# Attention's keys loaded late in the projections, and stores placed behind the last visit

## The chip, the cores and the metric

The kernel runs on one core of a Trainium2 chip. The metric is the device time in microseconds of one launch. Engines are named as in the profile: PE is TensorE (PEld its weight loads), DVE VectorE, ACT ScalarE, POOL GpSimd, SP SyncE; SPq and ACTq are the instruction queues of SP and ACT, from which DMAs are issued.

## What is computed

A transformer block with conditioning: 2048 tokens, width 512, 32 heads of 16, a hidden layer of 1792, all in float32.

```python
mod = silu(c) @ w_mod                      # six vectors: sa, ca, ga, sb, cb, gb
h = layernorm(x) * (1 + ca) + sa
q, k, v = split(h @ wqkv)                  # 32 heads of 16
p = softmax(q @ k.T / 4)                   # per head, 2048 x 2048
x = x + ga * ((p @ v) @ wo)
h = layernorm(x) * (1 + cb) + sb
out = x + gb * (gelu(h @ w1 + b1) @ w2 + b2)
```

## The kernel before

Heads are worked on in eight groups of four, tokens in four blocks of 512. One group with one block of queries is a unit `u` (32 in all). Float32 products are made of a rounded high part and a low remainder, so a projection of a block is 12 matmuls of 512 columns in `mm3` (line 303). Its `fill` list holds functions that are called between these 12 matmuls: with three entries, after matmuls 4, 8 and 12.

**First part** (to about 72 us). The loop over blocks `b` normalizes a block, transposes it, and makes the queries and keys of the first quarter of the heads (`proj_qk` with `k = 0`) and some rows of values (`proj_v`). Each projection returns a function `rest` that issues the store of its result to device memory (lines 456, 459, 481); it is called after the matmuls of the next projection. The queue that issues it is `st[0]`. At first that is ACT.

**Second part** (about 72 to 299 us). 33 projections are left, numbered here 0 to 32: nine of values and 24 `proj_qk` with `k` from 1 to 3. Between their matmuls run 97 *visits*, numbered 0 to 96. A visit computes score products for the softmax maxima of nine units, before attention starts: six matmuls (line 566, tiles `mx<-kt,qmx`), half of them read out by ACT (line 572) and half by DVE (line 575). Visits read queries from `qmx` (two buffers, six DMAs of 64 KB each per unit, line 508) and combined keys from `kt0` or `kt1` (`build_k`, line 497, six DMAs of 256 KB). The units come in the order 0, 1, 2, 3, 4, 5, 8, 6, 7. Visit 42 is the first of unit 4, visit 64 the first of unit 8, visit 74 the first of unit 6, visit 85 the first of unit 7. Unit 8 belongs to another group of heads, so `kt0` is built anew for it, from `kpm1` in device memory, which `pair_store` (line 456) writes after projections 11 and 15.

**Attention** (299 to 1404 us) needs `kq0`, the plain keys of the first heads (again six DMAs of 256 KB), and in each key tile four rows of ones (`one_rows`, line 533, two DMAs of 32 KB over two partitions). The rest of the time goes to the feed-forward layers.

All loads, and from projection 1 on all stores, are issued by SP, one after another in the order in which the code was written. A DMA is issued when its data and its buffer are ready, and, since there are eight completion counters which the DMAs take in turn, when the earlier DMA on its counter has landed. So a DMA that waits holds up all that stand behind it in SP's queue. Engines run their instructions in the order of the code too; nothing is reordered.

Of the kernel before, what the change touches and what calls it, by code (L numbers as in the profile page):

```python
# [35 lines left out]

FRONT = (0, 1, 2, 3, 4, 5, 8, 6, 7, 9)
NU1 = len(FRONT) - 1
VISIT = 3
OP0 = 1  # L40
OPN = 4
# [11 lines left out]
def block_kernel(ctx: ExitStack, tc: tile.TileContext, x, wqkv, wo, w1, b1, w2, b2, c, w_mod, out):  # L53
    nc = tc.nc
    te, ve, ac, gp, sy = nc.tensor, nc.vector, nc.scalar, nc.gpsimd, nc.sync
    ctx.enter_context(tc.manual_schedule())

    def pool(name, bufs=1, **kw):
        cm = tc.tile_pool(name=name, bufs=bufs, **kw)
        return cm, cm.__enter__()  # L60

    def close(cm):
        cm.__exit__(None, None, None)
# [86 lines left out]
    def load_x(b):  # L150
        for t in range(4):
            r0 = b * TB + t * P
            sy.dma_start(x_tile(b, t), x[r0 : r0 + P, :])
# [4 lines left out]
    def load_w(k, hold=lambda raw: None):  # L158
        if k < 4:
            raw = tpool.tile([P, 2, KC, P], F32, tag="wraw", name="wraw")  # L160
            hold(raw)
            for w in (1, 0):
                sy.dma_start(raw[:, w], wq_r[:, :, w * D + k * P : w * D + (k + 1) * P])
        else:
            raw = vraw
            hold(raw)
            for i in range(KC):
                sy.dma_start(raw[:, i], wq_r[:, i, 2 * D :])
        raws[k] = raw
# [5 lines left out]
    def split_w(k):  # L175
        raw = raws.pop(k)
        w_parts(k)
        for w in (1, 0):
            if k > 1:
                gp.tensor_copy(w_hi[k][:, w], raw[:, w])  # L180
            else:
                ac.activation(w_hi[k][:, w], raw[:, w], AF.Copy)
            gp.tensor_tensor(w_lo[k][:, w], raw[:, w], w_hi[k][:, w].bitcast(F32), op=ALU.subtract)
# [34 lines left out]
    def mod_cols(v, r, ps=None, f0=0, f1=KC):  # L218

        if ps is None:  # L220
            ps = bank()[:, : 2 * KC]
        for fc in range(f0, f1):
            te.matmul(ps[:, fc * 2 : fc * 2 + 2], r[:, fc * P : (fc + 1) * P], sel[:, :2], start=True, stop=True)
        p2 = ps.rearrange("p (f i) -> p f i", i=2)
        ve.tensor_scalar(modc[:, v, f0:f1, 0], p2[:, f0:f1, 0], 1.0, None, op0=ALU.add)
        ve.tensor_copy(modc[:, v, f0:f1, 1], p2[:, f0:f1, 1])

    def mod_store(r):

        ps = bank()  # L230
        te.matmul(ps[:2], sel[:, :2], r, start=True, stop=True)
        g = apool.tile([P, D], F32, tag="h32", name="grow", bufs=3)
        ac.activation(g[:2], ps[:2], AF.Copy)
        sy.dma_start(g_d, g[:2])
# [39 lines left out]
    def ln1(b):  # L274

        tiles = [x_tile(b, t) for t in range(4)]
        mv, rs = ln_stats(tiles)

        def rows():
            for t in range(4):  # L280
                ve.tensor_scalar(tiles[t], tiles[t], mv[:, t, 0:1], rs[:, t : t + 1],
                                 op0=ALU.subtract, op1=ALU.mult)
            return tiles

        return rows

    def ln1_t(b, tiles, between=lambda: None):
        hi = hpool.tile([P, KC, TB], FR, name=f"hThi{b}")
        lo = hpool.tile([P, KC, TB], FR, name=f"hTlo{b}")
        hT[b] = hi, lo  # L290
        tr, evac = transposed(tiles, hi, lo, 0, apool, lambda fc: bank_mx() if fc < KC - 1 else bank(), (ve, gp))
        pss = [tr(fc) for fc in range(KC - 1)]
        between()
        pss.append(tr(KC - 1))
        return lambda: [evac(fc, pss[fc]) for fc in range(KC)]
# [12 lines left out]
    st = [ac]  # L308
# [183 lines left out]
    def build_k(dst, src, g, t0=0, t1=S, parts=(0, 1, 2)):  # L492
        for i in parts:
            part = (0, 0, 1)[i]
            for a in range(2):
                r0 = a * 64 + i * DH
                sy.dma_start(dst[r0 : r0 + DH, :, t0:t1].bitcast(F32), heads(src, g, part, a, t0, t1))

    def load_k(g, tile):
        kst[g] = tile  # L500
        build_k(tile, qk_d[1][g // 2], g)
# [8 lines left out]
    def load_qm(u):  # L510

        qmx[u] = qmpool.tile([P, 2, TB], FR, tag="qmx", name="qmx", bufs=2)
        build_q(u, qmx[u])
# [16 lines left out]
    def one_rows(k):  # L530
        for a in range(2):
            r0 = a * 64 + KR
            sy.dma_start(k[r0 : r0 + 2].bitcast(F32), one_d[:, None, :].to_broadcast([2, 2, S]))

    mxs, left, vabs = {}, {}, {}

    mi = [NU1 * NM, NU1 * NM]

# [80 lines left out]
    rest = lambda: None  # L619

    def proj(f, *args):

        nonlocal rest
        r = f(*args)
        rest()
        rest = r

    for b in range(NB):
        if b == NB - 1:
            close(lcm)  # L630
            kcm, kpool = pool("kpool")
            kts = [kpool.tile([P, 2, S], FR, name=f"kt{i}") for i in range(2)]
            qmcm, qmpool = pool("qmpool")
            kpm[0], kpm[1] = kts
            load_qm(0)
            build_k(kts[0], kpm_d[0], 0, 0, 2 * TB)
            load_qm(1)
        if b:
            if b + 1 < NB:
                xn = ln1(b + 1)()  # L640
            if b + 2 < NB:
                load_x(b + 2)
        proj(proj_qk, b, 0, 1, (), None if b else first[1])
        if b == 1:
            load_w(1)
        if b == NB - 1:
            st[0] = sy
            rest()
            rest, st[0] = lambda: None, ac
            split_w(1)  # L650
        proj(proj_qk, b, 0, 0, (), None if b else first[0])
        if b == 0:
            xn = ln1(1)()
        if b == NB - 1:
            mod_store(mrow)
            break
        if b == 1:
            mod_cols(1, mrow)
        for _ in range(V_A[b][0]):
            proj(proj_v, *vitems.pop(0), (), len(vitems) == 15)  # L660
        ev = ln1_t(b + 1, xn)
        ev()
        for _ in range(V_A[b][1]):
            proj(proj_v, *vitems.pop(0))
        if b < 2:
            mrow = mod_rows(wms)
        if b == 0:
            wms = [load_wm(2, 0), load_wm(5, 1)]
# [8 lines left out]
    items = [(None, b, t) for b, t in vitems] + [(k, b, w) for k in range(1, 4) for b in range(NB) for w in (1, 0)]  # L677
    nv = len(vitems)

    half = [("V", 0), None]  # L680
    for n in range(1, 16 * NU1):
        half += [("V", n), ("U", n - 1)]
    half += [None, ("U", 16 * NU1 - 1)]
    slots = list(zip(half + [None], [None] + half))
    visits = -(-len(slots) // VISIT)
    led, todo = 0, []
    new = []

    def visit():
        nonlocal led  # L690
        for sl in slots[led : led + VISIT]:
            for a in range(2):
                if sl[a]:
                    new.extend(half_slot(*sl[a], a))
        led += VISIT

    for n, (k, b, w) in enumerate(items):
        if n == 1:
            close(acm)
            st[0] = sy  # L700
        if n == 0:
            build_k(kts[0], kpm_d[0], 0, 2 * TB, S)
        if n == 5:
            load_w(2)
        if n == 7:
            build_k(kts[1], kpm_d[0], 1)
            for t in kts:
                one_rows(t)
        if n == nv + 1:
            close(vwcm)  # L710
            kqcm, kqpool = pool("kqpool")
            kq = [kqpool.tile([P, 2, S], FR, name="kq0")]
            one_rows(kq[0])
            vgcm, vgpool = pool("vgpool", bufs=2)
            qcm, qpool = pool("qpool")
        if n == nv + 2:
            load_k(0, kq[0])
        if n == nv + 10:
            kpm[2] = kts[0]
            build_k(kts[0], kpm_d[1], 2)  # L720
        if n == nv + 15:
            load_v(0)
        if n == nv + 19:
            load_k(2, kts[0])
        if n == nv + 18:
            load_q(0)
        if n == nv + 20:
            load_q(1)
        if k and b == 1 and w and k < 3:
            split_w(k + 1)  # L730
            if k + 2 < 4:
                load_w(k + 2)
        new = []
        nm = len(items)
        fill = [lambda rest=rest: (rest(), visit())] + [visit] * (visits * (n + 1) // nm - visits * n // nm - 1)
        if n == len(items) - 1:
            fill += [lambda: None] * 2
        rest = proj_qk(b, k, w, fill) if k else proj_v(b, w, fill)
        for f in todo[:1]:
            f()  # L740
        todo = todo[1:] + new
# [386 lines left out]
```

## Time and profile before

| | us |
|---|---|
| median of 3 runs | 1750.71 |
| the three runs | 1748.58, 1750.71, 1758.66 |
| time of the profiled execution | 1758.06 |
| its span | 1756.2 |
| PE busy | 1741.6 (99%) |
| mean granted PE clock | 0.987 |

The profiled execution is 7.35 us above the median. Times in the rows count from the start of the span; the program's remaining 1.86 us lie around it. PE is busy nearly all the time, and a busy PE can still be a slow one: the granted clock tells. The chain of waits names PE for 94% of the span.

### The profile page before, as it was taken

The page shows a single profiled execution, that of the slowest core. Times are in us where ns is not written, and L with a number is a line of the kernel's source. Part 1 is how long each engine was busy: PE and PEld are TensorE (multiplying, and loading weights), DVE is VectorE, ACT ScalarE, POOL GpSimd, SP SyncE. Part 2 cuts the span into 40 slices and gives each one's busy share as a digit, 9 for nine tenths or more (in the row PEclk, how much of TensorE's full clock was granted, in tenths as well). Part 3 has the DMA queues.
Part 4 walks back from the last instruction along what each step waited for, and adds up shares of the span by engine and source line. Part 5 has one row for each costly group of instructions (what it writes and reads, how often), then busy time and mean ns, then how long its engine had stood idle before and what let it go on. Part 6 is the DMA issues. An engine that isn't in the chain of part 4 may idle for free.

```text
span 1756.2 us, 28900 instructions
## 1 busy us (share of the span) xinstructions
PE 1741.6 (99%) x10560; PEld 907.7 (52%) x10560; DVE 1395.9 (79%) x2563; ACT 1352.2 (77%) x2582; POOL 317.8 (18%) x347
## 2 busy tenths in 40 slices
PE   9999999999999999999999999999999999999999
PEld 7665555334343433434334343343433388888887
DVE  6698869898888888888888888888886286746553
ACT  3587758999999999999999999999999722222322
POOL 3205513010000000000000000000003254645562
PEclk9999969999999999999999999999999999999999
DMA  8758627811400410410410101101113064424341
GB/s 306 226 113 193 155 86 160 126 35 29 87 23 23 81 28 24 74 36 23 74 31 27 39 23 36 38 23 32 27 49 116 19 192 133 138 72 120 97 120 48
DMA packets 125219, 144.15 MB, mean 82 GB/s; under 512 B 39027, under 2 KB 74867, under 8 KB 123125
## 3 DMA queue, kind: packets, MB, share of 16 engines
q1 hardware_dynamic: 121620, 135.21, 31.0%
q10 hardware_dynamic: 3456, 7.10, 1.1%
q8 instruction: 83, 1.36, 0.3%
q14 instruction: 60, 0.48, 0.1%
HBM read 106.37 MB, written 35.87 MB: 81 GB/s over the span
## 4 chain that ended last, share of the span: by engine, by line
PE 94%; DVE 2%; DMA 2%; POOL 0%; issue 0%; ACT 0%; SPq 0%; ACTq 0%; POOLq 0%; DVEq 0%
PE pv L796 29%; PE mx L547 20%; PE sc L303 14%; PE sc L963 13%; PE mx L1027 6%; PE mx L566 5%; PE pv L1027 2%; PE sc L903 2%; PE mx L903 1%; DMA qk<-parts 1%; DMA kq<-qk 1%; PE pv L343 0%; DMA qmx<-qk 0%; PE sc L260 0%; PE sc L356 0%
## 5 line engine op out<-in xcount | busy, mean ns | idle before, releaser
L964 ACT ACTIVATE p<-sc 128x512 f32<-128x512 f32 x2048 | 1054.7, 613 | 38.6 <-PE sc L963 13.6
L549 DVE TENSOR_REDUCE mxs<-mx 128x1 f32<-128x512 f32 x1472 | 927.8, 684 | 112.8 <-PE sc L963 87.5
L796 PE MATMUL pv<-p,vg 128*32 128x512 f32 x4096 | 546.0, 605 | 0.0
L963 PE MATMUL sc<-qst,kq 50*128 50x512 f32 x1024 | 284.2, 435 | 0.8 <-ACT raw L434 0.8
L963 PE MATMUL sc<-qst,kt 50*128 50x512 f32 x1024 | 282.0, 431 | 0.0
L547 PE MATMUL mx<-kq,qmx 48*128 48x512 f32 x768 | 261.7, 428 | 0.2
L547 PEld LDWEIGHTS mx<-kq,qmx 48*128 48x128 f32 x768 | 122.5, 184 | 228.6 <-DVE mxs L549 209.3
L547 PE MATMUL mx<-kt,qmx 48*128 48x512 f32 x704 | 239.8, 427 | 0.0
L547 PEld LDWEIGHTS mx<-kt,qmx 48*128 48x128 f32 x704 | 113.4, 184 | 208.5 <-DVE mxs L549 190.7
L575 DVE CUSTOM_DVE_ANT_0 cp<-mx,cp 128x512 f32<-128x512 f32 x288 | 183.8, 688 | 39.2 <-PE mx L566 36.5
L1006 ACT ACTIVATE g<-sc,b_c 128x512 f32<-128x512 f32 x56 | 38.6, 690 | 223.1 <-PE sc L303 218.6
L572 ACT ACTIVATE cp<-mx 128x512 f32<-128x512 f32 x288 | 151.6, 599 | 57.1 <-PE mx L566 57.0
L588 POOL CAST m<-mn 128x16 fp32r<-128x16 f32 x32 | 6.3, 198 | 1025.2 <-DVE mn L582 1025.2
L796 PEld LDWEIGHTS pv<-p,vg 128*32 128x32 f32 x4096 | 81.0, 108 | 180.5 <-issue 168.8
L963 PEld LDWEIGHTS sc<-qst,kq 50*128 50x128 f32 x1024 | 125.7, 185 | 32.7 <-ACT p L964 23.8
L1010 DVE TENSOR_TENSOR glo<-g,ghi 128x512 fp32r<-128x512 f32 x56 | 57.5, 1027 | 92.2 <-ACT ghi L1009 92.2
L963 PEld LDWEIGHTS sc<-qst,kt 50*128 50x128 f32 x1024 | 125.6, 185 | 9.6 <-ACT p L964 3.1
L566 PE MATMUL mx<-kt,qmx 48*128 48x512 f32 x576 | 106.1, 465 | 6.0 <-DMA qmx<-qk 2.9
L832 POOL TENSOR_TENSOR w1l<-w1r,w1h 128x512 fp32r<-128x512 f32 x56 | 76.5, 1366 | 146.7 <-DVE w1h L831 123.1
L566 PEld LDWEIGHTS mx<-kt,qmx 48*128 48x128 f32 x576 | 57.6, 200 | 55.9 <-DVE mxf L575 19.3
L834 POOL TENSOR_TENSOR w2l<-w2r,w2h 128x512 fp32r<-128x512 f32 x56 | 82.5, 1474 | 6.2 <-DVE w2h L833 5.8
L303 PE MATMUL sc<-hThi,w 128*128 128x512 f32 x240 | 77.4, 450 | 0.7 <-DVE hThi L266 0.7
(175 smaller groups left out, 1677.6 us busy)
## 6 DMA issues: line engine op xcount, KB each, us to landing
w1r<-in_B_w_dram SPq DMA_DIRECT2D x56, 256.0 KB
w2r<-in_B_w_dram SPq DMA_DIRECT2D x56, 256.0 KB
qk<-parts SPq DMA_DIRECT2D x25, 512.0 KB
qmx<-qk SPq DMA_DIRECT2D x192, 64.0 KB
qst<-qk SPq DMA_DIRECT2D x192, 64.0 KB
kq<-qk SPq DMA_DIRECT2D x24, 256.0 KB
kt<-qk SPq DMA_DIRECT2D x24, 256.0 KB
vg<-v SPq DMA_DIRECT2D x8, 664.0 KB
```

Source lines behind the costliest of these rows:

```text
L303: te.matmul(ps, p, q, start=i == 0, stop=i == len(terms) - 1)
L547: te.matmul(ps, qmx[u][rows, p, qc * P : (qc + 1) * P], kst[u // NB][rows, p, kr * TB : (kr + 1) * TB], start=True, stop=True)
L549: ve.tensor_reduce(mxs[u][:, p, a, qc, kr : kr + 1], ps, axis=AX.X, op=ALU.max, negate=True)
L566: te.matmul(ps, qmx[u][rows, p, qc * P : (qc + 1) * P], kpm[u // NB][rows, p, t0 : t0 + TB], start=True, stop=True)
L572: ac.activation(vabs[n, a], ps, AF.Abs)
L575: ve.tensor_tensor_reduce(v, ps, v, -0.5, 3.0e38, ALU.add, ALU.min, mxs[u][:, p, a, qc, r : r + 1])
L796: te.matmul(cur_pv[0][32 * j : 32 * (j + 1)], vg[g][:, kc, j * VW : j * VW + 32], pt.pop((s, j)), start=kc == 0, stop=kc == NKC - 1)
L832: gp.tensor_tensor(alo, a, ahi.bitcast(F32), op=ALU.subtract)
L834: gp.tensor_tensor(blo, b, bhi.bitcast(F32), op=ALU.subtract)
L963: te.matmul(ps, k[r0 : r0 + KX, p, kc * P : (kc + 1) * P], q[r0 : r0 + KX, p], start=True, stop=True)
L964: ac.activation(pb, ps, AF.Exp, scale=SCALE)
L1027: te.matmul(acc[qb][t], p[:, sl], q, start=f == 0 and n == 0, stop=f == NF - 1 and n == 2)
```

## The change

The change does four things.

- **Stores of the first part.** `st[0]` becomes SP from the second `proj_qk` of block 1 on (before: from projection 1 of the second part, with one store of block 3 as an exception). Ten stores move from ACT's queue to SP's.
- **Keys and ones of attention.** `kq0` is loaded at the start of projection 22 (`nv + 13`) and not of projection 11. The rows of ones of `kt0`, `kt1` and `kq0` are loaded at the start of projection 23, and not at 7 and 10.
- **Stores of the second part.** In `fill`, `rest` is called just ahead of the last visit of the next projection, and no longer ahead of its first.
- **Visits.** Projection 0 has none; the 97 are spread over projections 1 to 32. Projections 1 to 31 have three each and 32 has four. Before, two projections had two and 31 had three.

```diff
+FILL0 = 1
...
         if b == 1:
             load_w(1)
+            st[0] = sy
         if b == NB - 1:
-            st[0] = sy
             rest()
-            rest, st[0] = lambda: None, ac
+            rest = lambda: None
             split_w(1)
...
         if n == 1:
             close(acm)
-            st[0] = sy
...
             build_k(kts[1], kpm_d[0], 1)
-            for t in kts:
-                one_rows(t)
...
-            one_rows(kq[0])
...
-        if n == nv + 2:
+        if n == nv + 13:
             load_k(0, kq[0])
+        if n == nv + 14:
+            for t in (kq[0], *kts):
+                one_rows(t)
...
-        nm = len(items)
-        fill = [lambda rest=rest: (rest(), visit())] + [visit] * (visits * (n + 1) // nm - visits * n // nm - 1)
+        fill = [rest]
+        if n >= FILL0:
+            m, nm = n - FILL0, len(items) - FILL0
+            fill = [visit] * (visits * (m + 1) // nm - visits * m // nm - 1) + [lambda rest=rest: (rest(), visit())]
```

Three places in SP's queue show what moves. A row gives the line, the tile written and the one read, and the shape; a `<-` from `qk`, `kpm`, `one` or `m` is a load, a row that writes one of these is a store (`qk10` to `qk13` hold keys, `qk00` to `qk03` queries). Lines of the changed kernel are higher by one or two.

First place, SP at the end of the first part. Before:

```order
L163 DMA wraw_605<-in_A_wqkv_dram 128x4x128 x2
L508 DMA qmx_833<-qk00_83 16x2x512 x6
L497 DMA kt0_828<-kpm0_91 16x2x1024 x6
L508 DMA qmx_846<-qk00_83 16x2x512 x6
L459 DMA qk10_87<-parts_866 128x2x512
```

The changed kernel, from the same row on:

```order
L164 DMA wraw_605<-in_A_wqkv_dram 128x4x128 x2
L460 DMA qk10_87<-parts_592 128x2x512
L457 DMA kpm0_91<-pmh_596 128x2x512
L457 DMA kpm0_91<-pmh_597 128x2x512
L460 DMA qk00_83<-parts_621 128x2x512
L482 DMA v_137<-vst4_183 128x664
L482 DMA v_137<-vst0_179 128x664
L460 DMA qk10_87<-parts_748 128x2x512
L460 DMA qk00_83<-parts_767 128x2x512
L509 DMA qmx_833<-qk00_83 16x2x512 x6
L498 DMA kt0_828<-kpm0_91 16x2x1024 x6
L509 DMA qmx_846<-qk00_83 16x2x512 x6
```

Eight of the ten stores now stand ahead of the loads of the first visits, which before were on ACT's queue.

Second place, SP ahead of the queries of visit 42 (`qmx_1875`, now `qmx_1880`). Before:

```order
L533 DMA kq0_1724<-one_139 2x2x2048 x2
L459 DMA qk11_88<-parts_1715 128x2x512
L497 DMA kq0_1724<-qk10_87 16x2x2048 x6
L163 DMA wraw_1825<-in_A_wqkv_dram 128x4x128 x2
L459 DMA qk01_84<-parts_1810 128x2x512
L508 DMA qmx_1875<-qk00_83 16x2x512 x6
L459 DMA qk11_88<-parts_1919 128x2x512
```

The changed kernel:

```order
L460 DMA qk11_88<-parts_1664 128x2x512
L164 DMA wraw_1771<-in_A_wqkv_dram 128x4x128 x2
L460 DMA qk01_84<-parts_1762 128x2x512
L509 DMA qmx_1880<-qk00_83 16x2x512 x6
L460 DMA qk11_88<-parts_1858 128x2x512
```

The keys `kq0` and their ones no longer stand ahead of these queries.

Third place, SP around visit 64, for which `kt0` is built from `kpm1` and the queries are `qmx_2518`, now `qmx_2528`. Before:

```order
L459 DMA qk12_89<-parts_2434 128x2x512
L508 DMA qmx_2518<-qk01_84 16x2x512 x6
L456 DMA kpm1_92<-pmh_2283 128x2x512
L456 DMA kpm1_92<-pmh_2284 128x2x512
L497 DMA kt0_828<-kpm1_92 16x2x2048 x6
L459 DMA qk02_85<-parts_2530 128x2x512
```

The changed kernel, as far as the queries of visit 74 (`qmx_2843`):

```order
L460 DMA qk12_89<-parts_2401 128x2x512
L457 DMA kpm1_92<-pmh_2229 128x2x512
L457 DMA kpm1_92<-pmh_2230 128x2x512
L498 DMA kt0_828<-kpm1_92 16x2x2048 x6
L509 DMA qmx_2528<-qk01_84 16x2x512 x6
L460 DMA qk02_85<-parts_2484 128x2x512
L460 DMA qk12_89<-parts_2591 128x2x512
L596 DMA m4_109<-mt_2516 32x32 x4
L460 DMA qk02_85<-parts_2673 128x2x512
L498 DMA kq0_1678<-qk10_87 16x2x2048 x6
L460 DMA qk12_89<-parts_2760 128x2x512
L509 DMA qmx_2843<-qk00_83 16x2x512 x6
```

The store and the load of unit 8's keys now stand ahead of its queries, and the keys `kq0` stand ahead of the queries of visit 74.

## The prediction

> **What bounds the kernel.** First the page: span, chain, granted clock in 40 slices of 43.9 us.
>
> ```profile
> span 1756.2 us, 28900 instructions
> PE 1741.6 (99%) x10560; PEld 907.7 (52%) x10560; DVE 1395.9 (79%) x2563; ACT 1352.2 (77%) x2582; POOL 317.8 (18%) x347
> PEclk9999969999999999999999999999999999999999
> PE 94%; DVE 2%; DMA 2%; POOL 0%; issue 0%; ACT 0%; SPq 0%; ACTq 0%; POOLq 0%; DVEq 0%
> ```
>
> PE carries the end, so only two things can shorten the time: PE idling less, or PE running faster while busy. The one slice at 6 (219 to 263 us) shows the second. Next the second part in windows, cut where PE idles and where the clock changes.
>
> ```profile
> core 0: us, PE busy (x) PEld busy (x) DVE busy (x) ACT busy (x) POOL busy (x), PEclk, DMA share, GB/s
> 161.90:164.90 3.00, 0.13 (x4) 0.06 (x2) 1.24 (x4) 0.98 (x2) 1.46 (x2) 0.94 1.07 294
> 164.90:171.40 6.50, 6.50 (x18) 3.62 (x20) 2.80 (x9) 2.66 (x5) 1.57 (x5) 0.50 0.94 342
> 171.40:213.20 41.80, 41.80 (x204) 25.35 (x204) 38.33 (x122) 34.24 (x66) 23.01 (x25) 1.00 0.58 132
> 213.20:215.80 2.60, 0.53 (x4) 0.29 (x3) 0.45 (x2) 0.62 (x2) 1.83 (x2) 0.99 0.93 199
> 215.80:253.30 37.50, 37.47 (x107) 20.44 (x104) 20.41 (x65) 18.15 (x35) 6.13 (x9) 0.50 0.35 117
> 253.30:299.00 45.70, 45.70 (x217) 26.77 (x217) 42.83 (x137) 37.04 (x72) 14.20 (x18) 1.00 0.66 151
> ```
>
> Twice PE does almost nothing for some 2 to 3 us while the DMA engines are full, and each time the granted clock is 0.50 right after: for 6.50 us, and for 37.50 us. In these 44.0 us PE counts as busy, and it gets through 107 matmuls in 37.50 us, against 217 in 45.70 us later. The chain gives the price. One round is four matmuls of a projection (sc) and one visit (mx), at full and at half clock:
>
> ```profile
> 206.05 1.13 PE sc L303 x4
> 207.18 0.94 PE mx L566 x6
> ...
> 224.66 2.00 PE sc L303 x4
> 226.66 1.58 PE mx L566 x5
> ```
>
> 2.07 us against 3.58 us: of every us at half clock 1 − 2.07/3.58 = 0.42 us is lost. So the 44.0 us cost 44.0 × 0.422 = 18.6 us, more than the idle time that precedes them. The question is whether the change removes both idles.
>
> **First idle: visit 42.** The chain, then PE's and SP's timelines (start, duration, what, and the idle before it):
>
> ```profile
> 146.97 9.93 DMA kq<-qk
> 156.90 0.02 issue
> 156.91 7.30 DMA qmx<-qk
> ...
> 164.87 0.79 PE L566 MATMUL mx<-kt,qmx 48*128 48x512 f32 x2 [2.87 <-DMA qmx<-qk]
> ...
> 144.04 4.28 SPq L497 DMA_DIRECT2D kq<-qk  x6
> 152.73 8.62 SPq L508 DMA_DIRECT2D qmx<-qk  x6
> ```
>
> The six keys `kq0` were issued from 144.04 us on and the last landed at 156.90, so one takes (156.90 − 144.04)/6 = 2.14 us. Six queries behind them needed 8.62 us to be issued, since each waited for a landing ahead. The change takes these keys and the two loads of ones out from ahead of them. Then I expect the six issues to take what they take at 193.15 us (2.66, below), 6 us less, and the idle was 2.87. It goes, with its 6.50 us of half clock.
>
> **Second idle: visit 64.** PE, then SP:
>
> ```profile
> 215.41 2.09 PE L566 MATMUL mx<-kt,qmx 48*128 48x512 f32 x6 [2.07 <-issue]
> ...
> 180.04 11.46 SPq L459 DMA_DIRECT2D qk<-parts  x3
> 191.14 0.36 SPq L459 DMA_DIRECT2D qk<-parts  x1
> 193.15 2.66 SPq L508 DMA_DIRECT2D qmx<-qk  x6
> 195.86 0.94 SPq L456 DMA_DIRECT2D kpm<-pmh  x2
> 201.03 2.65 SPq L497 DMA_DIRECT2D kt<-kpm  x6
> ```
>
> `kt0` of unit 8 can be loaded only after the two stores of `kpm1` (195.86) have landed; SP stood from 196.80 to 201.03 for it, and six loads of 2.14 us then land at about 201.03 + 12.8 = 213.9. The stores themselves stood behind queries that waited until 193.15. In the changed order they come right after the store that ends here at 191.50: 4.36 us earlier, so the keys are there at about 213.9 − 4.4 = 209.5, or 211.9 if the store two rows ahead still ends late. The visit wanted them at 215.41 − 2.07 = 213.34, and now stands four matmuls later in its projection, 1.13 us, at 214.5. Spare 2.6 to 5.0 us. The queries of the visit now come behind these keys. Six of 64 KB take 3.2 us at the keys' 122 GB/s (256 KB in 2.14 us), and 1.0 us at the rate of this window in which stores land:
>
> ```profile
> 217.00:219.00 2.00, 2.00 (x7) 1.16 (x4) 1.16 (x5) 1.08 (x2) 0.40 (x2) 0.50 1.05 404
> ```
>
> By the larger they land between 212.7 and 215.1, by the smaller between 210.5 and 212.9. I take 213.4 us, spare 1.1, as they are small and follow one another without a wait. So this idle goes too, more narrowly than the first, and with it 2.07 us and 37.50 us of half clock.
>
> **What moves into the gap: `kq0` ahead of visit 74.** The keys land behind the queries of visit 64 and ahead of those of visit 74, ten rounds or 10 × 2.07 = 20.7 us later, plus the spare of 1.1: 21.8 us. In it have to land two stores of 512 KB (1.3 us each at 404 GB/s), four small ones and a third large store (together 0.7 + 1.3), six keys (12.8) and six queries (1.0 to 3.2, I take 1.5): 18.9 us, at most 20.6. Spare 1.2 to 2.9 us, which is the tightest place. A store in this stretch that waits for its data, like the three at 180.04, can take it. The loads of ones (six small DMAs) come behind these queries and hold nothing that is wanted within the next visits; I cost them at nothing, covered by the eleven visits (23 us) up to visit 85, and at six issues of 0.44 us, 2.7 us of SP, without that cover.
>
> **Stores of the first part, and the first visit.** PE's idles there, ACT's wait, and SP's and DVE's rows around them:
>
> ```profile
> 49.95 2.12 ACT L265 ACTIVATE h<-mx,modc 128x512 f32<-128x512 f32 x3 [1.31 <-DMA v<-vst]
> ...
> 54.68 0.73 PE L303 MATMUL sc<-hThi,w 128*128 128x512 f32 x2 [0.47 <-DVE hThi L266]
> 59.90 1.33 PE L260 MATMUL mx<-ident,xin 128*128 128x128 f32 x7 [0.35 <-DVE xin L281]
> ...
> 74.59 1.01 PE L566 MATMUL mx<-kt,qmx 48*128 48x512 f32 x3 [1.02 <-DMA kt<-kpm]
> ...
> 41.38 4.06 SPq L163 DMA_DIRECT2D wraw<-in_A_wqkv_dram  x2
> 62.07 3.26 SPq L508 DMA_DIRECT2D qmx<-qk  x6
> ...
> 60.21 1.28 DVE L442 TENSOR_TENSOR parts<-sc,parts 128x512 fp32r<-128x512 f32 x2
> ```
>
> ACT was blocked 1.31 us behind a store's issue on its own queue; the products that wait for the normalized block idled 0.47 and 0.35 us. With the stores on SP, which has nothing from 45.44 to 62.07 us, ACT goes on. The gain lies between 0 (DVE is late by itself) and 0.82; I take 0.8, as ACT's wait is longer than the idles behind it. SP pays eight issues (two of the ten stores come later) of about 0.4 us, 3.2 us, in 16.6 free us, and holds only the first visits' loads: the last of these stores needs its data, ready at about 61.5 us (DVE's row), so the queries at 62.07 hardly move. The first visit waited 1.02 us for `kt0`. Projection 0 has no visits now, so it is wanted some 2.3 us later (two blocks of four matmuls, 2 × 1.13): the 1.02 us go, unless the stores push the keys back by over 1.3 us, which leaves 0 as the other end.
>
> **Visits and `rest`.** 97 visits stay 97. The last projection has four, and its rounds have fewer projection matmuls:
>
> ```profile
> 294.54 0.70 PE sc L303 x2
> 295.23 1.18 PE mx L566 x6
> ```
>
> This round of two and six takes 1.88 us, where half of 1.13 and 0.94 would make 1.51; what holds it back I take to be the reading out by DVE and ACT. That costs 0 to 4 × 0.37 = 1.5 us; I take 0.5, since projection 0 gets shorter by what it gave away. The `rest` is only an issue on SP; placed two visits later it delays nobody but what stands behind it on SP, counted above.
>
> **Sum**, against the profiled execution of 1758.06 us (span 1756.2 and 1.86 around it), which is 7.35 above the median of the runs: 1758.06 − 18.6 (half clock) − 2.87 − 2.07 (idles) − 1.02 (first visit) − 0.8 (first part) + 0.5 (last projection) = **1733.2 us**. The half clock is not there any more, however long it was in the other runs, so I do not subtract the 7.35 again. If they have another cause than the clock, the result is 1725.8: the low end. Against 1750.71 the forecast is −1.0%; about 0.5% (8.8 us, so 1741.9 to 1759.5) is what a measurement tells from no change.
>
> **Rivals.**
>
> *The half clock is short in most runs.* Here two idles of 2.87 and 2.07 us were each followed by half clock, once for 6.50 and once for 37.50 us with PE busy for 37.47. If every run but the profiled had 6.50 us twice, the change takes from 1750.71: 2 × 6.50 × 0.422 + 4.94 + 1.32 = 11.7, so 1739 us. For it: the timed runs differ by 10 us among themselves. Against it: then the profiled execution should lie 31 × 0.422 = 13 us above the median, not 7.35. [...] 8%.
>
> *A new wait at visit 74, or still at 64,* behind the keys `kq0`: over 2 us of idle if one more large load or a late store falls into the 18.9 us. It costs 2.5 us and again half clock of 6.50 to 37.50 us (2.7 to 15.8 us): 1738 to 1751 us. For it the spare of 1.2 to 2.9 us. Against it: the idle of 1.02 us at 74.59 shows that a small miss is only its own length. 14%.
>
> *The change does not do what it says at visit 64:* the stores of `kpm1` wait for their data as before, and the long half clock stays. Then 1750.71, less at most 7.4 (2.87 and 6.50 × 0.422 of the first idle, 1.8 at the front), and plus what the tighter queue gives back: 1743 to 1751. For it the 11.46 us that the three stores at 180.04 took. 6%.
>
> *The other side: the DMA queue becomes the bound.* From 161.9 to 299 us the DMA shares add up to 3.2 + 6.1 + 24.2 + 2.4 + 13.1 + 30.2 = 79 us of full engines in 137 us. Without the idles and the half clock the stretch is 114 us, and `kq0` brings 12.8 us more: 92 in 114, 81%. If transfers that follow closer take over 20% longer, each set of queries is late, PE idles again and again, and the clock stays at half from visit 64 on: 33 rounds × 1.51 = 50 us, 1783 us. Against it: windows at 294 to 404 GB/s show the queue faster than what is asked. 4%.
>
> **How the numbers follow.** 68% for the sum, its own range 1725 to 1739. Faster by over 0.5%: 68 + 8 + half of the 14 = 83%; within: 7 + 6 = 13%; slower: 4%. The range 1725 to 1747 takes in the first rival and most of the second; about 1 in 10 is left out beside what the terms of the sum may miss.
>
> **What would show it.** In the changed kernel: no window at 0.50 between 150 and 275 us; no idle over 1 us ahead of L567 at visits 42, 64 and 74; six query issues of visit 42 in about 2.7 us; SP's wait between the `kpm1` store and `kt0` unchanged near 4 us, but ending ahead of the queries; no ACT wait on a store of `v`; attention starting near 274 us and not 299. Wrong it is if PE idles over 2 us anywhere in the second part, or if half clock turns up without an idle ahead of it.

## The result, and the profile after

| | before | changed |
|---|---|---|
| median of the runs, us | 1754.68 | 1731.18 |
| lowest to highest, us | 1748.58 to 1764.15 | 1729.91 to 1734.43 |
| profiled execution, us | 1758.06 | 1731.22 |
| its span, us | 1756.2 | 1729.4 |
| its mean granted clock | 0.987 | 0.999 |

The ratio is 0.9862, with a 95% interval from 0.9826 to 0.9897: faster, by 1.4%. The sum of the prediction was 1733.2 us, and the changed kernel's median lies 2.0 us below it. The two profiled executions differ by 26.84 us, where the sum had 24.9. The changed kernel is also steadier: its runs lie within 4.5 us, those of before within 15.6.

The page of the changed kernel, the lines that answer to those of before:

```profile
span 1729.4 us, 28903 instructions
PE 1721.2 (100%) x10560; PEld 898.5 (52%) x10560; DVE 1394.4 (81%) x2563; ACT 1351.9 (78%) x2582; POOL 317.6 (18%) x347
PEclk9999999999999999999999999999999999999999
PE 96%; DMA 2%; DVE 1%; ACT 0%; SPq 0%; POOL 0%; issue 0%; ACTq 0%; POOLq 0%
```

PE does the same 10560 matmuls in 20.4 us less busy time, and no slice is below nine tenths of the clock. The second part in windows (the columns are those of the prediction's windows):

```profile
core 0: us, PE busy (x) PEld busy (x) DVE busy (x) ACT busy (x) POOL busy (x), PEclk, DMA share, GB/s
140.00:180.00 40.00, 40.00 (x197) 24.13 (x196) 38.07 (x121) 34.20 (x67) 27.31 (x32) 1.00 0.38 128
180.00:220.00 40.00, 39.94 (x197) 24.09 (x196) 37.67 (x122) 33.30 (x65) 16.93 (x21) 1.00 0.94 168
220.00:260.00 40.00, 40.00 (x197) 23.79 (x194) 37.42 (x121) 33.74 (x66) 12.67 (x17) 1.00 0.81 182
```

In these 120 us PE is idle for 0.06 us in all, although the DMA engines are busy at a share of 0.94 for 40 us on end. PE's timeline at visits 0, 42, 64 and 74 and at attention's start, then SP's:

```profile
73.87 0.73 PE L567 MATMUL mx<-kt,qmx 48*128 48x512 f32 x3
159.87 0.96 PE L567 MATMUL mx<-kt,qmx 48*128 48x512 f32 x6
205.34 0.96 PE L567 MATMUL mx<-kt,qmx 48*128 48x512 f32 x6
225.79 1.07 PE L567 MATMUL mx<-kt,qmx 48*128 48x512 f32 x6
272.96 0.84 PE L965 MATMUL sc<-qst,kq 50*128 50x512 f32 x3 [0.77 <-ACT raw L435]
...
140.44 3.56 SPq L509 DMA_DIRECT2D qmx<-qk  x6
181.47 1.39 SPq L457 DMA_DIRECT2D kpm<-pmh  x2
186.68 2.85 SPq L498 DMA_DIRECT2D kt<-kpm  x6
189.59 9.16 SPq L509 DMA_DIRECT2D qmx<-qk  x6
206.22 3.33 SPq L498 DMA_DIRECT2D kq<-qk  x6
```

No wait stands at visits 0, 42, 64 and 74. The only idle over 0.35 us that is left, from 20 us to the last matmul, is the 0.77 us at attention's start. The kernel before has it as well:

```profile
299.87 0.83 PE L963 MATMUL sc<-qst,kq 50*128 50x512 f32 x3 [0.77 <-ACT raw L434]
```

Attention starts at 272.96 us (before 299.87; forecast 274), and from there to the end both kernels take the same: 1756.2 − 299.87 = 1456.3 us, and 1729.4 − 272.96 = 1456.4. So the whole gain lies ahead of attention. The stores of `kpm1` are issued 23.9 us ahead of visit 64 (205.34 − 181.47), where they were 17.5 us ahead (213.34 − 195.86). The queries of visit 64 took 9.16 us to be issued, more than those that stopped PE at visit 42 in the kernel before (8.62). So a long time on the queue is not yet a wait of PE. What counts is whether the data land before the matmul that reads them.

### The profile page after: what moved, and what is told of

It reads as the page before. It is cut to its first block, busy times and chain, and to the rows that moved or that the text cites. A ratio compares the mean times of both kernels' runs of the same rounds, so it can differ in the third digit from the quotient of the medians.

```text
span 1729.4 us, 28903 instructions
## 1 busy us (share of the span) xinstructions
PE 1721.2 (100%) x10560; PEld 898.5 (52%) x10560; DVE 1394.4 (81%) x2563; ACT 1351.9 (78%) x2582; POOL 317.6 (18%) x347
## 4 chain that ended last, share of the span: by engine, by line
PE 96%; DMA 2%; DVE 1%; ACT 0%; SPq 0%; POOL 0%; issue 0%; ACTq 0%; POOLq 0%
PE pv L798 29%; PE mx L548 20%; PE sc L304 16%; PE sc L965 13%; PE mx L1029 6%; PE mx L567 5%; PE pv L1029 2%; PE sc L905 2%; PE mx L905 1%; DMA kt<-kpm 1%; PE sc L261 0%; PE sc L205 0%; PE sc L357 0%; DMA wmod<-in_w_mod_dram 0%; DMA qk<-parts 0%; DMA kpm<-pmh 0%
## 5 line engine op out<-in xcount | busy, mean ns | idle before, releaser
L548 PE MATMUL mx<-kt,qmx 48*128 48x512 f32 x704 | 239.7, 427 | 0.0
L567 PE MATMUL mx<-kt,qmx 48*128 48x512 f32 x576 | 97.7, 433 | 0.1
L304 PE MATMUL sc<-kt,w1h 128*128 128x512 f32 x224 | 73.8, 391 | 0.0
```

What stands on the lines that cost most here:

```text
L304: te.matmul(ps, p, q, start=i == 0, stop=i == len(terms) - 1)
L548: te.matmul(ps, qmx[u][rows, p, qc * P : (qc + 1) * P], kst[u // NB][rows, p, kr * TB : (kr + 1) * TB], start=True, stop=True)
L567: te.matmul(ps, qmx[u][rows, p, qc * P : (qc + 1) * P], kpm[u // NB][rows, p, t0 : t0 + TB], start=True, stop=True)
```

## Experiments

The theory was: two idles of PE, each from late loads, and the half clock that each brings. The questions are: which of the four parts takes the idles away, and is it the idle that lowers the clock?

### The parts one by one

Every fence with an edit shows it against the kernel before, unless the text names the changed kernel. `...` and `(...)` stand for lines and words left out. The time at half clock of a run is worked out as 2 × (1 − mean granted clock) × span, as the traces of both kernels record no granted clock but 1.00 and 0.50; it is given as the mean over a kernel's runs. The experiments ran on three chips, each with runs of the kernel before beside them, whose medians are 1754.7 to 1757.5 us. The ratio is to those on the same chip; the interval in it, and not a difference of medians across rows, tells what is clear of the spread.

| parts made | median, us | ratio to before (95%) | at half clock, us |
|---|---|---|---|
| none | 1754.7 | | 39 to 44 |
| stores behind the last visit | 1755.3 | 0.9993 (0.996 to 1.0026) | 39 |
| first stores on SP | 1743.1 | 0.9930 (0.9898 to 0.9962) | 21 |
| keys and ones late | 1741.7 | 0.9929 (0.9893 to 0.9965) | 16 |
| visits from projection 1 | 1733.7 | 0.9875 (0.9861 to 0.9890) | 3 |
| visits from 1, stores behind | 1733.9 | 0.9868 (0.9820 to 0.9917) | 2 |
| visits from 1, first stores | 1733.5 | 0.9852 (0.9806 to 0.9898) | 3 |
| all but the late keys | 1733.2 | 0.9867 (0.9853 to 0.9882) | 4 |
| all four | 1731.2 | 0.9862 (0.9826 to 0.9897) | 3 |

**Keys and ones late, alone.**

```diff
-            for t in kts:
-                one_rows(t)
...
-            one_rows(kq[0])
...
-        if n == nv + 2:
+        if n == nv + 13:
             load_k(0, kq[0])
+        if n == nv + 14:
+            for t in (kq[0], *kts):
+                one_rows(t)
```

> The kernel before with one part of the change: the plain keys kq0 and the rows of ones loaded late (projections 22 and 23). By the prediction the queries of visit 42 are no longer behind keys: the idle of 2.87 us and the 6.50 us at half clock after it go, 5.6 us in all, while the second idle (visit 64, 2.07 us) and its half clock stay, so about 1749 us against a before of 1754.7. Rival, the keys are what makes visit 64 late too: both idles go, about 1732 us, clock 1.00. Rival, the first idle has another cause (the store ahead of the queries): nothing changes, 1754 us.

PE's idles between 130 and 230 us, the window behind them, and SP's issue of visit 42's queries:

```profile
209.81 0.70 PE L566 MATMUL mx<-kt,qmx 48*128 48x512 f32 x3 [0.99 <-DMA kt<-kpm]
210.74 0.70 PE L566 MATMUL mx<-kt,qmx 48*128 48x512 f32 x3 [0.24 <-DMA kt<-kpm]
211.50:222.00 10.50, 10.50 (x31) 5.78 (x32) 5.70 (x20) 5.34 (x11) 2.30 (x4) 0.51 1.08 189
145.09 4.61 SPq L508 DMA_DIRECT2D qmx<-qk  x6
```

The first idle is gone, so taking the keys out from ahead of the queries is enough for visit 42. Visit 64 still waits, 1.23 us in all, and half clock follows. The time fell by 13 us and not by 5.6. The half clock of these runs is 16 us on average, against 39 in the runs of before on the same chip: at 0.42 per us that is 9.5 us, and the idles are 3.7 us shorter in the profiled executions (2.87 and 2.07 against 1.23). I had expected the half clock at visit 64 to stay as long as it was; why it got shorter the runs do not show.

**Stores behind the last visit and visits from projection 1, together.**

```diff
+FILL0 = 1
...
-        nm = len(items)
-        fill = [lambda rest=rest: (rest(), visit())] + [visit] * (...)
+        fill = [rest]
+        if n >= FILL0:
+            m, nm = n - FILL0, len(items) - FILL0
+            fill = [visit] * (...) + [lambda rest=rest: (rest(), visit())]
```

> The kernel before with another part alone: stores behind the last visit of the next projection, and no visits in projection 0; keys, ones and first stores as before. By the prediction the second idle goes with its long half clock (2.07 + 15.8 us) and the first visit's wait of 1.02 us, the first idle stays with 6.50 us of half clock: about 1736 us, clock near 0.998. Rival, visit 64 needs the late keys too: both idles stay, about 1754 us.

1733.9 us, and no idle over 0.2 us between 130 and 230 us. My expectation that the first idle would stay was wrong: visit 42 does not wait although the keys stand ahead of its queries. So these two edits were taken apart.

**Stores behind the last visit, alone** (as above with `FILL0 = 0`).

> The kernel before with the stores behind the last visit of the next projection, the visits spread over all 33 projections as before. If the stores' place is what frees visit 64: no idle there, while the first visit's 1.02 us and the first idle of 2.87 us with some 7 to 14 us of half clock stay: 1738 to 1742 us. If the later visits are what helps: both idles stay, 1750 us or more.

**Visits from projection 1, alone** (as above with `FILL0 = 1`, and `rest` ahead of the first visit as before).

> The kernel before with no visits in projection 0 and 97 in the other 32, the stores ahead of the first visit as before. Visit 42 then stands 8 matmuls (2.3 us) later against the projections and visit 64 stands 4 (1.1 us) later, so of the idles of 2.87 and 2.07 us some 0.6 and 0.9 us are left, and the first visit's 1.02 us goes. If idles under 1 us do not lower the clock: clock 1.00, about 1736 us. If they do at times: some runs at 0.99, median 1738 to 1745 us. If the place of the stores is what counts: second idle and its half clock stay, 1750 us.

The stores alone bring nothing, the visits alone nearly all. PE and SP with the stores moved:

```profile
164.27 0.80 PE L567 MATMUL mx<-kt,qmx 48*128 48x512 f32 x2 [2.56 <-DMA qmx<-qk]
216.74 0.70 PE L567 MATMUL mx<-kt,qmx 48*128 48x512 f32 x3 [2.56 <-issue]
194.01 2.66 SPq L509 DMA_DIRECT2D qmx<-qk  x6
196.71 0.94 SPq L457 DMA_DIRECT2D kpm<-pmh  x2
201.78 2.66 SPq L498 DMA_DIRECT2D kt<-kpm  x6
```

and with the visits moved (the first PE row is visit 42):

```profile
162.17 0.96 PE L567 MATMUL mx<-kt,qmx 48*128 48x512 f32 x6
207.81 0.97 PE L567 MATMUL mx<-kt,qmx 48*128 48x512 f32 x6 [0.20 <-issue]
138.59 3.44 SPq L498 DMA_DIRECT2D kq<-qk  x6
149.35 8.60 SPq L509 DMA_DIRECT2D qmx<-qk  x6
183.78 1.39 SPq L457 DMA_DIRECT2D kpm<-pmh  x2
188.94 2.85 SPq L498 DMA_DIRECT2D kt<-kpm  x6
192.32 10.52 SPq L509 DMA_DIRECT2D qmx<-qk  x6
```

With the stores moved, both idles are there (2.56 us each) and SP's order is that of before: queries, then `kpm1`'s stores, then `kt0`. With the visits moved `kpm1`'s stores and `kt0` stand ahead of the queries of visit 64. The reason is in the code: the queries of a unit are loaded from inside a visit (`load_qm` in `half_slot`), while stores and keys are issued by the projections. Visits that start one projection later make all their loads of queries later in SP's queue, behind the stores and keys of the same projection, and are themselves due 4 to 8 matmuls later. At visit 42 the queries still stand behind the keys and take 8.60 us to be issued (before 8.62). But the keys are issued from 138.59 us on (before 144.04). The query that visit 42 waits for therefore landed at 161.20 us, 1.5 us ahead of its matmul, where before it landed 2.7 us after the matmul could have begun (164.67 against 162.00). So the change in `fill` that starts the visits one projection later did both.

**First part's stores on SP, alone.**

```diff
         if b == 1:
             load_w(1)
+            st[0] = sy
         if b == NB - 1:
-            st[0] = sy
             rest()
-            rest, st[0] = lambda: None, ac
+            rest = lambda: None
```

> The kernel before with the third part alone: ten stores of the first part on SP in place of ACT. By the prediction ACT's wait of 1.31 us on a store goes and PE's idles of 0.47 and 0.35 us with it, 0.8 us, while the first visit still waits about 1 us or a little more for its keys, and both later idles stay: within 2 us of before, whose spread is larger, so the trace decides. Rival, the stores push the loads of the first visits back by over 1 us: the first visit waits 2 us or more, and half clock follows there.

The first part in windows, then the first visit, visit 42, the half clock behind it, and visit 64:

```profile
40.00:60.00 20.00, 20.00 (x115) 15.59 (x114) 17.82 (x39) 9.07 (x16) 5.93 (x6) 1.00 0.89 326
60.00:71.50 11.50, 11.50 (x49) 7.97 (x47) 7.35 (x13) 6.57 (x12) 3.89 (x4) 1.00 0.82 174
72.03 0.46 PE L566 MATMUL mx<-kt,qmx 48*128 48x512 f32 x1 [0.48 <-DMA kt<-kpm]
162.52 0.50 PE L566 MATMUL mx<-kt,qmx 48*128 48x512 f32 x2 [2.76 <-DMA qmx<-qk]
163.50:177.00 13.50, 13.50 (x40) 7.24 (x38) 7.02 (x24) 6.19 (x13) 2.30 (x4) 0.50 0.67 225
215.08 1.54 PE L566 MATMUL mx<-kt,qmx 48*128 48x512 f32 x6 [1.03 <-DVE mxf L575]
```

From 40 to 71.5 us PE has no idle, and the first visit starts at 72.03 us, 2.6 us earlier than before, after a wait of 0.48 us for its keys. The median is 11.6 us below that of before, more than these 2.6 us and more than the 2 us that I had expected. The half clock of these runs is 21 us on average against 39, which at 0.42 per us is 7.3 us more. The half clock after visit 42 lasted 13.65 us here, where in the profile of before it lasted 6.83; the visits ran slower for longer, visit 64 waited 1.03 us only, and no half clock followed there. One reading is that a long half clock after the first idle gives the loads of the second time to arrive. It is not shown, and the run with the stores moved speaks against it: 10.24 us of half clock followed its wait at visit 42, and visit 64 still waited 2.56 us.

**Two parts: visits from projection 1 and the first stores.** The edits are shown above.

> The kernel before with two parts of the change: no visits in projection 0, and the first part's stores on SP; keys, ones and the stores of the second part as before. If these two are all that counts: 1731 to 1732 us, clock 0.999, as the changed kernel (no visits in projection 0 alone gave 1733.7, and the stores 2 to 3 us up to the first visit). If the late keys or the place of the stores bring something of their own: 1734 us or more, or an idle over 1 us at visit 42 or 64.

**All but the late keys** (the changed kernel, with `load_k` and `one_rows` back in their old places).

> The changed kernel with one part undone: kq0 loaded at projection 11 again and the ones at 7 and 10. The prediction as written needs the late keys for the first idle: it comes back with its half clock, 2.87 + 2.7 us, about 1737 us. Rival, from the run with the stores and visits moved alone, in which visit 42 did not wait although the keys stood ahead of its queries: the later visits are enough, no idle over 1 us anywhere, 1730 to 1732 us, clock 0.999 or more, and moving the keys is worth nothing in the changed kernel.

1733.5 and 1733.2 us, and no idle over 0.2 us between 130 and 230 us in either. The intervals of these kernels and of the changed one cover each other, so what the late keys and the stores' place add in the changed kernel can't be told from nothing, and no kernel here was faster than it by more than that.

What the late keys do change is where the spare lies. The trace gives it as the time from the landing of the query load that the visit's first matmul on the new unit needs to the start of this matmul:

| parts made | visit 42, us | visit 64, us | visit 74, us |
|---|---|---|---|
| visits from projection 1 | 1.5 | 0.2 | 14 |
| all but the late keys | 3.5 | 0.7 | 15 |
| all four | 15 | 0.2 | 0.1 |

A matmul that did wait began 0.2 us after the landing (164.87 after 164.67 at visit 42 before), so 0.2 and 0.1 us mean just in time. With the late keys visit 42 has ample room, but visit 74 has none left. The kernel with all parts but the late keys has the same time within the spread and is further from a new wait.

### The idle and the clock

**The idles filled.** The kernel before, with matmuls on data already there.

```diff
+DUMMY = {64: 10, 96: 7}
...
+        if kind == "V" and a == 0 and n in DUMMY:
+            w = FRONT[v - 1]
+            for _ in range(DUMMY[n]):
+                te.matmul(ps, qmx[w][rows, 1, 3 * P :], kts[1][rows, 1, 3 * TB :], start=True, stop=True)
         te.matmul(ps, qmx[u][rows, p, qc * P : (qc + 1) * P], kpm[u // NB][rows, p, t0 : t0 + TB],
```

> The kernel before, its loads as late as before, but PE is given something to do where it idled: 10 extra matmuls on data already there ahead of the first matmul of visit 42, and 7 ahead of visit 64, into the bank that the visit's own matmul overwrites. If the idle lowers the clock: no half clock, clock 1.00, 18.6 us less or about 1736 us, the waits themselves still there but filled. If the half clock comes from the heavy DMA traffic that stands around both idles: windows at 0.50 stay, and the time is that of before or up to 4 us more. [...]

The extra matmuls (L570) ahead of visit 42 and what is left of the idle, then the windows that were at half clock before:

```profile
162.20 2.46 PE L570 MATMUL mx<-kt,qmx 48*128 48x512 f32 x10
165.05 0.50 PE L571 MATMUL mx<-kt,qmx 48*128 48x512 f32 x2 [0.40 <-issue]
165.00:171.50 6.50, 6.45 (x32) 3.69 (x32) 4.73 (x16) 4.22 (x9) 2.98 (x5) 1.00 0.93 340
214.20:254.00 39.80, 39.80 (x194) 24.00 (x194) 37.11 (x119) 33.31 (x65) 12.28 (x16) 1.00 0.49 156
```

The loads are as late as before and the traffic is as dense (0.93 at 340 GB/s), but in this execution the clock stays at 1.00 in both places. So dense traffic alone did not lower the clock here; nor did it in the changed kernel, where the share is 0.94 over 40 us at a clock of 1.00. The median is 1745.4 us and not 1736, since the runs still had 17 us of half clock on average (39 without fillers). Where it lay in the runs without a profile is not recorded.

**More of it** (`DUMMY = {64: 18, 96: 14}`).

> The kernel before with 18 and 14 extra matmuls in place of 10 and 7 ahead of visits 42 and 64, enough for the longest idle seen there. If idle PE is all that lowers the clock there: runs at 0.997 and more but for the idle of 0.77 us at attention's start, mean half clock under 10 us where 10 and 7 extra matmuls left 17 and none 39 to 44; about 1741 to 1744 us, as the extra matmuls outlast the waits by 1 to 3 us. If the traffic or something else lowers it: the mean half clock stays at 17 us or more, 1747 us.

1746.0 us, above the 1741 to 1744 expected, with 10.8 us at half clock on average: a quarter of the 44 that the kernel before had beside it, and between the two values that were to decide (under 10, and 17 or more). The profiled execution shows something that the theory does not allow:

```profile
162.71 3.83 PE L570 MATMUL mx<-kt,qmx 48*128 48x512 f32 x16
166.16 0.49 PE L571 MATMUL mx<-kt,qmx 48*128 48x512 f32 x1
163.00:166.50 3.50, 3.50 (x18) 2.82 (x17) 1.02 (x4) 0.76 (x2) 1.90 (x2) 1.00 0.98 248
166.50:177.00 10.50, 10.50 (x31) 5.78 (x30) 4.72 (x15) 4.24 (x8) 2.31 (x4) 0.51 0.70 255
```

PE has no idle, and the clock falls right behind 3.83 us that held hardly anything but fillers. A filler has the form 48*128, where a matmul of a projection has 128*128, and runs by itself, where a visit's matmuls start in pairs (in the trace of before two at 161.27 us, the next two at 161.60 and 161.61): six of a visit took 0.94 us, 10 fillers 2.46. So idle PE was not all that lowered the clock here. It may be too little work on PE, of which idle is one form; or the traffic, at a share of 0.98, may play a part when there is little work. No run with fillers of the form 128*128 was made, so this stays open.

**A wait put back into the changed kernel.** After `build_k(kts[0], kpm_d[1], 2)`, part of `kt0` is read again, so that the queries of visit 64 come later: 128 KB, 256 KB, or twice 256 KB.

```diff
+            sy.dma_start(kts[0][:DH].bitcast(F32), heads(kpm_d[1], 2, 0, 0, 0, S))
```

> The changed kernel with 128 KB more to read ahead of the queries of visit 64, half of what gave an idle of 1.93 us there: about 0.9 us of idle. If the clock falls by chance, more often the longer the idle (1.93 us: three runs of five): one run in four or fewer below 0.997, median 1731 to 1734 us. If every idle under 1 us is harmless: all runs at 0.998 or more, 1732 us. If the length of the idle does not matter: as with 256 KB, about 1743 us.

> The changed kernel with one more load of 256 KB (one part of kt0 read a second time) between the keys and the queries of visit 64. The queries there landed only about 0.1 us ahead of the visit, so PE should idle about 2 us. If such an idle lowers the clock: half clock of 7 to 38 us behind it in most runs, 1736 to 1749 us, clock 0.989 to 0.998. [...] If my spare of 1.1 us was right: an idle of 1 us, 1732 us.

> The changed kernel with 512 KB more ahead of those queries: about 4 us of idle at visit 64. If the clock falls by chance, more often the longer the idle: every run below 0.998, 1735 us (4 us of idle alone) plus 3 to 15 us, median 1742 to 1748 us. If the length of the half clock depends on the idle: 0.986 or less in every run, 1750 us and more. [...]

The edit shown is that for 256 KB. Visit 64 with 128, 256 and 512 KB, and the half clock behind the last two:

```profile
205.74 0.96 PE L567 MATMUL mx<-kt,qmx 48*128 48x512 f32 x6 [0.67 <-DMA qmx<-qk]
207.35 1.19 PE L567 MATMUL mx<-kt,qmx 48*128 48x512 f32 x6 [1.93 <-DMA qmx<-qk]
208.00:228.60 20.60, 20.60 (x60) 11.32 (x58) 11.73 (x38) 10.29 (x20) 4.21 (x6) 0.50 0.94 160
210.08 1.65 PE L567 MATMUL mx<-kt,qmx 48*128 48x512 f32 x6 [5.31 <-DMA qmx<-qk]
210.00:222.50 12.50, 12.42 (x37) 7.02 (x37) 6.81 (x22) 6.03 (x12) 2.31 (x4) 0.50 1.06 205
```

| idle at visit 64 in the profiled execution, us | median, us | mean granted clock of the runs |
|---|---|---|
| none | 1731.2 | 0.998 to 1.000 |
| 0.67 | 1733.4 | 0.998 to 1.000 |
| 1.93 | 1742.9 | 0.990, 0.993, 0.993, 0.999, 1.000 |
| 5.31 | 1747.7 | 0.988 to 0.998, all ten below 0.999 |

So a wait put back by itself brought the half clock back. The longer the idle, the more often the clock fell: at 1.93 us in three runs of five, at 5.31 us in at least nine of ten. The tenth is at 0.998, where runs without this idle lie too. The length of the half clock did not go by the idle: in the profiled executions it is 20.5 us behind 1.93, and 13.7 us behind 5.31. Being busy did not end it at once either: PE was busy for all of 20.60 us at half clock behind 1.93, and for 12.42 of 12.50 us behind 5.31.

## Why the prediction was right, point by point

- **The half clock, −18.6.** PE's busy time fell by 20.4 us, where the sum had 18.6 − 0.5 = 18.1 net. By the trace 49 matmuls of projections and 73 of visits ran at half clock. They took 500 and 272 ns each of PE's busy time, where such matmuls take 281 and 158 at full clock: 19.1 us. The other 1.3 us are spread over matmuls at full clock. The price of 0.42 holds across runs: 25 runs of the kernel before on one chip reach from 1744.98 us at a clock of 0.997 to 1767.15 us at 0.981, which is 22.2 us for 2 × 0.016 × 1754 = 56 us more at half clock, or 0.40 per us. PE's idle time fell by 6.4 us (1756.2 − 1741.6 against 1729.4 − 1721.2), where the sum had 6.8.
- **The base.** I took the profiled execution's time and did not subtract the 7.35 us by which it lay above the median. That was right: the spread of the kernel before is its half clock, and the changed kernel has hardly any to spread (0.998 to 1.000).
- **The first idle, −2.87.** It went, but the step that credits the late keys with it was only half right: they are enough for it and not needed, as without them the later visits do the same. I read the cause from what stood ahead of the queries, and did not count that visit 42 itself moved by 8 matmuls, as I had done for visit 64. The six issues took 3.56 us (I said 2.66), but from 140.44 us on (before 152.73).
- **The second idle, −2.07.** The order read from the queue was right (`kpm1`'s stores ahead of the queries), but it came from the later visits and not from the new place of the stores. The spare was too large: 1.1 us by my working, while the last query that the visit's first matmul reads landed at 205.10 us, and the visit began at 205.34: 0.2 us. The bounds had reached it, as by the larger price of a query they came at 215.1 for 214.5. At visit 74 I had 1.2 to 2.9 us; there the first matmul to read the new queries is the visit's fifth, at 226.36, and the last that it reads landed at 226.27: 0.1 us. That neither place waits noticeably is luck, not the spare of the forecast.
- **The first visit, −1.02:** gone.
- **The first part, −0.8.** Mis-sized: in the kernel before PE is idle for 0.83 us between 40 and 60 and 0.38 between 60 and 72 us, 1.21 in all, and other profiled executions with the same first part show 1.2 to 1.9 (1.17 at one place alone). In the changed kernel PE is busy for all of these 32 us. I had summed the two rows that I looked at, not the window, and took their sum for an upper bound.
- **The last projection, +0.5:** not measured by itself.
- **Rivals.** Half clock short in most runs: no, 39 to 44 us on average. A new wait at 74 or 64: it did not come, but was 0.1 and 0.2 us away. The runs with 256 KB more show its price: 1742.9 us, in the range of 1738 to 1751 that I gave. The DMA queue as the bound: its share rose to 0.94 over 40 us without a wait. The change not doing what it says: the stores did come early, though not by the edit that names them.

## What to carry to other kernels

Where one engine bounds a kernel, read its granted clock beside its busy time, and price a wait as its own length plus the half clock that the trace shows behind it: in the profiled execution before, 44.0 us of half clock stood behind 4.94 us of idle and cost some 19 us more. When loads come late for a consumer, ask what issues them: moving the consumer by a few matmuls moved its loads in the queue as well, and that alone gave 1733.7 us where all four parts gave 1731.2. Before crediting an edit, try it alone: two of the parts each removed the first idle by themselves, so neither was needed beside the other. And after a wait is gone, look at how closely it is missed: 0.1 us at visit 74 is no margin.

## What the chip showed unexpectedly

- Every stretch of half clock in these profiles, but for the one that the end of the program cuts off, lasted 1, 2, 3, 4, 6 or 11 times the shortest: 3.41 us (behind attention's start, idles filled), 6.83 (visit 42, before), 10.24 (visit 42, more fillers), 13.65 (visit 42, first stores on SP), 20.48 (visit 64, 256 KB more) and 37.55 us (visit 64, before), with PE busy nearly all through (37.47 of 37.50 us in the longest).
- The idle of 0.77 us at attention's start, which every kernel here has, was followed by half clock in 5 of the 14 profiled executions, and by none in 9; those of 0.8 to 1.1 us at the first visit, where there were any, by none. So whether a short idle lowers the clock differs from run to run; what decides it these runs do not show.
